# Two of eleven sums in an earlier place, and second readings of a weight in three tiles instead of one

## The chip, the core and the metric

The kernel runs on one core of one Trainium2 chip. The time is the device time of one execution, in microseconds (us). The kernel before took 561.12 us, the median of three runs (560.93 to 561.14). Beside the runs there is one execution recorded by the profiler, with a span of 558.1 us from the first to the last instruction.

The engines are named as in the profile: PE is TensorE (PEld are its weight loads), DVE is VectorE, ACT is ScalarE, POOL is GpSimd, and SP is the queue that issues most transfers. "L685" is line 685 of the kernel.

## What is computed

A gated recurrence over 768 tokens, for 4 batches of 8 heads of 48 values, then two matrix products with a SiLU between them, for 3072 tokens:

```python
for t in range(S):
    state = alpha[:, :, t, :, None] * state + np.einsum('bhd,bhe->bhde', k[:, :, t], v[:, :, t])
    y[:, :, t] = np.einsum('bhd,bhde->bhe', q[:, :, t], state)
...
x = np.ascontiguousarray(attn_out.transpose(0, 2, 1, 3)).reshape(B * S, H * D)   # 3072 x 384
h = x @ w_in                          # 384 x 2048
g = h * (1.0 / (1.0 + np.exp(-h)))
return (g @ w_out).astype(np.float32) # 2048 x 384
```

The weights arrive as 64-bit floats. The kernel reads them as pairs of 32-bit words and makes 32-bit floats of them.

## The kernel before

**Stages.** The tokens are cut into 24 pieces n of 128 (6 chunks of 4 batches), and four pieces form a group: six groups of 512 tokens. A loop of 25 steps, each with four slots, runs the attention of piece n (`scores`, `products`, `quotient`, `values`, `states`, `flip`, `land`). `values` writes the attention's output for two pieces side by side into a tile `xt`, one of the group's two halves. After each slot `fill` issues pieces of the two matrix products, as many as are due by a count of PE's work. A piece in the list `pieces` is a generator, its work, and the number of attention pieces that have to be done (`bridged`) before it may go. In the steps themselves the matmuls keep the order of the text on PE (`keep_in_program_order`); the operations of the other engines are ordered when the program is built, by their dependencies and their place in the text, and only those marked with `keep_in_program_order` stay behind what was written just ahead of them on their engine.

**First product.** `enter_plain` (groups 0 and 1) multiplies as the formula says. `enter` (groups 2 to 5) uses 20 block products in place of more (`PRODUCTS`, pairs of a combination of blocks of w_in and one of x), in seven pieces for each of two pairs of blocks. It needs combinations of blocks of x, which `sums_x` makes with the eleven operations of `SUMS_X` on VectorE; they lie in a tile `xc` of eleven rows, x numbers 6 to 16, of which the first sum writes x 9 and the second x 6. PE's first products of a group read x 9, x 6 and x 6, the fourth x 15, which is the eighth sum. The results are added up in VectorE (L944 and L998) and go through SiLU on ACT (L941).

**Second product.** `leave` takes g of half a group in seven pieces of 16 matmuls. VectorE or ACT add up the blocks and write the result o (L1042, L1040), which a DMA stores. Its two PSUM banks `ps_o` are used in turn.

**Order of pieces.** `both` puts the pieces of `leave` of one group and `enter` of the next in turns. `sums_x` of a group is a piece of no work at the head of its phase. The list `phases` says where a phase ends in `pieces`; `marks` says in which slot.

**Second readings.** `audit` reads alpha, w_in and w_out once more and reduces each piece to its largest (and for the weights smallest) value on VectorE (L685), for a test at the end of whether the fast way was allowed. It has 37 pieces: 9 of alpha (512 KB each), 12 of w_in (512 KB) and 16 of w_out (384 KB). All land in one tile, `bits` of the pool `look`, so that a transfer (L677) waits for the reduction of the one before. A call of the generator reduces one piece and asks for the next; two calls are made in each of the steps 15 to 24, the rest in the loop at L1215, which puts one or two pieces of the matrix products between two calls. Then come the test (`ends`, `good`, `small`, L1225 to L1236), with five pieces of the products in it, four more pieces, the load of the result into a register of each engine (L1239), hints for the branch (L1243), and the rest of the pieces. The slow way (`general`) is not entered.

**Tiles of attention.** `settle` allocates what is used from piece n = 8 on, when the tiles of the start are freed: `look`, `part`, `xc`, `turn`, `wx`, `p`, and the three tiles `at`, `kt` and `qt` (`late["quads"]`, 800 values in each of 128 partitions) into which alpha, k and q of a piece are loaded.

Of the kernel before, what the change touches and what calls it, by code (L numbers as in the profile page):

```python
# [8 lines left out]
F32 = mybir.dt.float32  # L9
I32 = mybir.dt.int32  # L10
# [9 lines left out]
def general(  # L20
# [322 lines left out]
SUMS_X = (  # L343
    (9, 1, 2, 1, 4), (6, 1, 0, 1, 2), (7, 1, 2, 1, 3), (8, 1, 0, 1, 7), (10, -1, 1, -1, 8),
    (11, 1, 5, -1, 10), (12, 1, 4, 1, 11), (15, -1, 0, 1, 12), (16, 1, 1, -1, 15),
    (13, 1, 4, 1, 7), (14, -1, 6, 1, 11),
)
# [8 lines left out]
def quotients(  # L356
# [19 lines left out]
    nc = tc.nc  # L376
    dve, act, gps = nc.vector, nc.scalar, nc.gpsimd

    late = {}
# [14 lines left out]
    B, H, S, D = q.shape  # L394
    C = 128
    NCH = S // C
    NP = H // 2
    HD = H * D
# [6 lines left out]
    GB = 4  # L405
# [3 lines left out]
    TB = GB * C // 2  # L409
    HO = HD // 2  # L410

    def pool(name, bufs=1, space=None):
        kw = {} if space is None else {"space": space}
        return ctx.enter_context(tc.tile_pool(name=name, bufs=bufs, **kw))
# [51 lines left out]
    def load(n, names="akq"):  # L466
        if n == NT:
            return
        c = ctxs.setdefault(n, dict(zip(("ci", "b"), divmod(n, B))))
        b, rows = c["b"], slice(c["ci"] * C, c["ci"] * C + C)  # L470
        for name, src in (("a", alpha), ("k", k), ("q", q)):
            if name not in names:
                continue
            x = src[b, :, rows, :]
            if n < NA:
                c[name] = nat[name][n % NIN]
                nc.sync.dma_start(c[name][:, :, 0:D], x.transpose([1, 0, 2]))
                continue

            c[name] = late["quads"][name]
            for u in range(2):
                for i in range(2):
                    r = 64 * u + 32 * i
                    nc.sync.dma_start(
                        c[name][r : r + 32, 32 * (1 - i) :][:, 0 : 4 * NP * D].rearrange(
                            "p (g c) -> p g c", g=NP),
                        x[u::2].rearrange("h (b j) d -> b h (j d)", j=4))
# [83 lines left out]
    quads = w_in.rearrange("p k (q i c) -> p i k q c", i=4, c=128)  # L573
# [6 lines left out]
    def combine(to, sa, a, sb, b):  # L580
        if sa == sb == 1:
            return dve.tensor_tensor(to, a, b, ALU.add)
        if sa == 1:
            return dve.tensor_tensor(to, a, b, ALU.subtract)
        if sb == 1:
            return dve.tensor_tensor(to, b, a, ALU.subtract)  # L586
        return dve.scalar_tensor_tensor(to, a, -1.0, b, ALU.mult, ALU.subtract)
# [69 lines left out]
    def audit():  # L657


        flat = alpha.rearrange("b h s d -> (b h s d)").rearrange("(p c) -> p c", p=128)  # L660
        todo = [(flat[:, c : c + AW], AW, 0) for c in range(0, flat.shape[1], AW)]
        if wide:
            todo += [(moe_w_in[t * 128 : t * 128 + 128, c : c + 512], 512, 1)
                     for c in range(0, DF, 512) for t in range(NKT)]
            todo += [(moe_w_out[f * 128 : f * 128 + 128, :], HD, 1) for f in range(NFT)]
        for kind in (0, 1):
            n = sum(x[2] == kind for x in todo)
            if n:
                seen.append([fix.tile([128, n], F32, name=f"seen{kind}{i}") for i in range(2)])
        at = [0, 0]  # L670
        for src, n, kind in todo:
            t = late["look"].tile([128, 512, 2], I32, name="bits")
            if kind == 0:
                x = t.rearrange("p n w -> p (n w)")[:, 0:n].bitcast(F32)
                nc.sync.dma_start(x, src)
            else:
                nc.sync.dma_start(t[:, 0:n, :].rearrange("p n w -> p (n w)"), src.bitcast(I32))  # L677
                x = t[:, 0:n, 1]
            yield
            i = at[kind]  # L680
            at[kind] += 1
            for which, op in ((0, ALU.max), (1, ALU.min)):
                if kind == 1 or which == 0:
                    tc.keep_in_program_order(
                        dve.tensor_reduce(seen[kind][which][:, i : i + 1], x, axis=AX, op=op,  # L685
                                          apply_absolute_value=True))

    xts, xcs = {}, {}
# [183 lines left out]
    def block_x(grp, at):  # L872

        if at < 2 * NKT:
            return xts[2 * grp + at % 2][:, at // 2, :]
        return xcs[grp][:, at - 2 * NKT, :]

    def sums_x(grp):
        xcs[grp] = late["xc"].tile([128, len(SUMS_X), TB], F32, name="xc")
        for to, sa, a, sb, b in SUMS_X:  # L880
            tc.keep_in_program_order(
                combine(block_x(grp, to), sa, block_x(grp, a), sb, block_x(grp, b)))
        yield
# [8 lines left out]
    turn = [0, 1, 2]  # L892
# [217 lines left out]
    def group(grp):  # L1110
        return [[(enter(grp, pair), 12, GB * grp + GB)] * 7 for pair in range(2)]

    def output(grp):
        return [[(leave(grp, h), 12, GB * grp + GB)] * 7 for h in range(2)]

    def both(x, y):
        for i in range(max(len(x), len(y))):
            pieces.extend(x[i : i + 1] + y[i : i + 1])

    pieces = []  # L1120
# [4 lines left out]
    phases = [len(pieces)]  # L1125
# [2 lines left out]
    phases.append(len(pieces))  # L1128
    before = output(1)
    for grp in range(2, NG):  # L1130
        pieces.append((sums_x(grp), 0, GB * grp + GB))
        for x, y in zip(before, group(grp)):
            both(x, y)
        phases.append(len(pieces))
        before = output(grp)
# [5 lines left out]
    def go_on():  # L1141

        nonlocal done
        next(pieces[done][0], None)
        done += 1

    audits = audit()
    done, bridged = 0, 0
    STEPS = NT + 1
# [4 lines left out]
    def settle():  # L1154

        first.close()
        late.update(look=pool("look"), part=pool("part"), xc=pool("xc"), turn=pool("turn"),
                    wx=pool("wx").tile([128, 8, NQ, 128], F32, name="wx"))
        quads = pool("quads")
        late["p"] = pool("p").tile([128, NP * W + 1], F32, name="p")  # L1160
        late["quads"] = {name: quads.tile([128, 32 + 4 * NP * D], F32, name=f"{name}t") for name in "akq"}
        for name, t in late["quads"].items():
            gps.memset(t, 1.0 if name == "a" else 0.0)
        load(NA)
# [20 lines left out]
    for step in range(STEPS):  # L1185
        if step == 1:
            load(NIN)
        stages = [[(scores, 1)], [(products, 0)], [(values, 1)], [(states, 1)]]
        if step == 1:

            stages = stages[1::-1] + stages[2:]
        elif step >= NA:
            stages = [[(land, 1), (scores, 1)], [(products, 0)], [(quotient, 0)],
                      [(values, 1), (states, 1), (flip, 0)]]
        for slot, group in enumerate(stages):
            for stage, lag in group:
                n = step - lag
                if not 0 <= n < NT:
                    continue
                stage(n)  # L1200
                if stage is values:
                    bridged = n + 1
                if stage is states and n + 1 + NIN < NA:
                    load(n + 1 + NIN)
                if stage is states and n + NV < NT:
                    load_v(n + NV)
            if step * SLOTS + slot == (NA + 1) * SLOTS - 1:
                x = decayed.rearrange("p (o i c) -> p o i c", o=2, c=C)
                for r, o in later:
                    gps.memset(x[r, o, :, 0:CH], 0.0)  # L1210
            fill(step, slot)
            if step * SLOTS + slot >= NA * SLOTS - 1 and conv_done[1] == NFT and not late:
                settle()
    turns = 0
    while next(audits, 0) is None:  # L1215
        turns += 1
        for _ in range(1 + turns % 2):
            go_on()

    checks = [(least.rearrange("p n j -> p (n j)"), ALU.min, 2.0**-64, ALU.is_gt),  # L1220
              (seen[0][0], ALU.max, 1.0, ALU.is_le)]
# [27 lines left out]
@with_exitstack  # L1249
def kernel(  # L1250
    ctx: ExitStack,
    tc: tile.TileContext,
    q: bass.AP,
    k: bass.AP,
    v: bass.AP,
    alpha: bass.AP,
    moe_w_in: bass.AP,
    moe_w_out: bass.AP,
    out: bass.AP,
):  # L1260


    flag = ctx.enter_context(tc.tile_pool(name="flag", bufs=1))
    small = flag.tile([1, 1], I32, name="small")
    args = (q, k, v, alpha, moe_w_in, moe_w_out, out)
    within = quotients(tc, small, *args)
    with tc.If(within < 1, label="general"):
        general(tc, *args)
# [30 lines left out]
```

## Time and profile before

| what | value |
|---|---|
| time, median of 3 runs | 561.12 us |
| span of the profiled execution | 558.1 us |
| mean clock granted to PE | 0.994 |
| DMA moved in the span | 70.13 MB, 126 GB/s |
| L685, max and min of a piece | 65 operations, 42.5 us busy, 24.0 us idle in front of them |
| L582 to L587 on xc, the sums of x | 44 operations |
| reductions of w_out | 455 to 518 us of the span |
| transfer of a piece of w_out, issue to landing | 3.1 us (median of 32) |
| L1239, load of the register | 479 to 535 ns on each engine |
| last store issued | 554.0 us, waited for until 556.2 us |

The span is that of the recorded execution. The runs contain about 3.0 us more, which lie outside the first and the last instruction. Busy shares are means over the whole span; the stages differ, so idle times are read from the timeline, stage by stage. A line of the timeline gives the start, the duration in us, the engine, the line, the operation, what it writes and reads with shapes, and in brackets the idle time of that engine in front of it with what ended it.

### The profile page before, as it was taken

How to read it: one execution, taken by the hardware profiler on the slowest of the kernel's cores; microseconds unless marked ns; L12 is line 12 of the kernel's file. 1: busy time of each engine (PE TensorE's matmuls, PEld its weight loads, DVE VectorE, ACT ScalarE, POOL GpSimd, SP SyncE). 2: the span in 40 equal slices, each digit the busy share in tenths (PEclk: the TensorE clock that was granted, in tenths of full speed). 3: DMA queues.
4: the chain of work that ended last, by engine and by line, in shares of the span. 5: the costliest groups of instructions: out<-in, count | busy, mean ns of one | idle time of the engine just before them, and what ended most of it. 6: DMA issues, size and time to landing. Idle time of an engine off the chain costs nothing. (4 is left out here: it accounts for less than half of the span.)

```text
span 558.1 us, 12640 instructions
## 1 busy us (share of the span) xinstructions
PE 541.4 (97%) x5026; PEld 488.8 (88%) x5026; DVE 445.1 (80%) x801; ACT 208.4 (37%) x466; POOL 75.9 (14%) x146
## 2 busy tenths in 40 slices
PE   5999999999999999999999999999999999999996
PEld 3788887998899898899999999988998999998996
DVE  5887889974999799997998986998894775857531
ACT  3456643223333243353353353353263341432200
POOL 4100010221211211021021021021121000001000
PEclk9799999999999999999999999999999999999999
DMA  9999861164445525355445654717712122333101
GB/s 218 255 276 177 232 189 40 38 164 108 126 131 136 142 62 134 88 145 157 129 109 142 194 141 115 198 22 179 180 48 84 53 99 95 111 109 106 38 25 32
DMA packets 99220, 70.13 MB, mean 126 GB/s; under 512 B 56272, under 2 KB 88656, under 8 KB 99152
## 3 DMA queue, kind: packets, MB, share of 16 engines
q1 hardware_dynamic: 97232, 65.30, 44.6%
q0 software_dynamic: 1920, 3.93, 2.0%
q8 instruction: 41, 0.67, 0.5%
q14 instruction: 27, 0.22, 0.1%
HBM read 61.34 MB, written 7.86 MB: 124 GB/s over the span
## 5 line engine op out<-in xcount | busy, mean ns | idle before, releaser
L388 PE MATMUL ps_o<-w_out,g 128*128 128x192 f32 x768 | 134.7, 329 | 1.1 <-DVE o L1042 0.9
L388 PEld LDWEIGHTS ps_o<-w_out,g 128*128 128x128 f32 x768 | 125.4, 190 | 5.1 <-DVE o L1042 2.3
L388 PE MATMUL ps_m<-xt,w_in 128*128 128x256 f32 x480 | 113.6, 383 | 1.5 <-ACT xt L851 1.1
L388 PEld LDWEIGHTS ps_m<-xt,w_in 128*128 128x128 f32 x480 | 89.1, 190 | 14.4 <-ACT xt L851 1.6
L388 PE MATMUL ps_o<-wt,g 128*128 128x192 f32 x576 | 99.7, 326 | 0.0
L388 PEld LDWEIGHTS ps_o<-wt,g 128*128 128x128 f32 x576 | 95.1, 190 | 1.6 <-issue 0.2
L388 PE MATMUL ps_m<-xc,w_in 128*128 128x256 f32 x288 | 70.7, 382 | 0.0
L685 DVE TENSOR_REDUCE seen<-bits 128x1 f32<-128x384 int32 (+2 forms) x65 | 42.5, 689 | 24.0 <-DMA bits<-in_moe_w_out_dram 19.6
L388 PEld LDWEIGHTS ps_m<-xc,w_in 128*128 128x128 f32 x288 | 53.6, 190 | 7.0 <-DVE g L944 0.3
L941 ACT ACTIVATE g<-g 128x1024 f32<-128x1024 f32 x32 | 33.0, 1056 | 59.0 <-DVE g L944 59.0
L1033 DVE TENSOR_TENSOR g<-g 128x512 f32<-128x512 f32 x72 | 49.8, 708 | 6.1 <-PE ps_o L388 6.1
L1045 POOL DMA_DIRECT2D out_dram<-o x40 | 22.0, 550 | 223.2 <-DVE o L1042 127.6
L813 POOL TENSOR_SCALAR_AFFINE_SELECT g<-g 64x256 f32<-64x256 f32 x64 | 34.2, 534 | 124.8 <-ACT g L806 105.8
L388 PE MATMUL ps_m<-xc,wx 128*128 128x256 f32 x192 | 50.0, 383 | 1.0 <-DVE xc L586 1.0
L936 ACT COPY g<-ps_m 128x512 f32<-128x512 f32 x64 | 36.5, 588 | 36.5 <-PE ps_m L388 36.4
L388 PEld LDWEIGHTS ps_m<-xc,wx 128*128 128x128 f32 x192 | 35.2, 190 | 5.3 <-ACT u L1064 1.3
L944 DVE TENSOR_TENSOR g<-ps_m,g 128x512 f32<-128x512 f32 x56 | 37.0, 684 | 2.9 <-PE ps_m L388 2.7
L722 DVE TENSOR_TENSOR_SCAN u<-al,one 128x516 f32<-128x516 f32 x24 | 30.0, 1249 | 10.6 <-ACT al L719 10.3
L909 ACT ACTIVATE g<-ps_m 128x512 f32<-128x512 f32 x32 | 19.1, 596 | 42.8 <-PE ps_m L388 42.3
L936 ACT COPY part<-ps_m 128x512 f32<-128x512 f32 x32 | 18.9, 589 | 43.0 <-DVE g L944 21.3
L752 DVE TENSOR_TENSOR_SCAN p<-al,inv 128x516 f32<-128x516 f32 x24 | 29.9, 1246 | 1.0 <-PE ps_a L388 0.4
L388 PE MATMUL ps_a<-g,vn 128*32 128x128 f32 x768 | 27.5, 278 | 1.8 <-POOL g L801 1.7
(126 smaller groups left out, 611.4 us busy)
## 6 DMA issues: line engine op xcount, KB each, us to landing
bits<-in_moe_w_in_dram SPq DMA_DIRECT2D x24, 512.0 KB, 4.8
bits<-in_moe_w_out_dram SPq DMA_DIRECT2D x32, 384.0 KB, 3.1
at<-in_alpha_dram SPq DMA_DIRECT2D x64, 96.0 KB, 2.5
kt<-in_k_dram SPq DMA_DIRECT2D x64, 96.0 KB, 2.5
qt<-in_q_dram SPq DMA_DIRECT2D x64, 96.0 KB, 2.6
bits<-in_alpha_dram SPq DMA_DIRECT2D x9, 512.0 KB, 3.8
out_dram<-o POOLq DMA_DIRECT2D x40, 96.0 KB, 2.4
flips<-turn SPq DMA_DIRECT2D x12, 256.0 KB, 2.4
```

Source lines behind the costliest of these rows:

```text
L388: in_order(nc.tensor.matmul(*args, **kw))
L685: dve.tensor_reduce(seen[kind][which][:, i : i + 1], x, axis=AX, op=op, apply_absolute_value=True))
L722: dve.tensor_tensor_scan(u[:, end - 1 :: -1], sg[:, end:0:-1], one[:, end:0:-1], 0.0, ALU.mult, ALU.add)
L752: dve.tensor_tensor_scan(p[:, 0:end], sg[:, 0:end], iv[:, 0:end], 0.0, ALU.mult, ALU.add)
L813: gps.affine_select(x, x, pattern=[[0, NP], [1, CH]], compare_op=ALU.is_ge, fill=0.0, base=0, channel_multiplier=-1)
L909: act.activation(gts[grp, h, pair][:, i : i + 2, q % 2, :], ps, AF.Silu)
L936: act.copy(to, ps)
L941: act.activation(x, x, AF.Silu)
L944: dve.tensor_tensor(to, a, b, op)
L1033: dve.tensor_tensor(cells(grp, h, pair, *to), cells(grp, h, pair, *x), cells(grp, h, pair, *y), ALU.subtract)
L1045: (gps if grp < NG - 1 else nc.sync).dma_start(out[r : r + C, c * HO : (c + 1) * HO], o)
```

## The change

`sums_x` is a generator with two parts now: it yields ahead of its third sum. The first part is a piece of its own, two places ahead of the end of the phase before, and may go when two of the group's four attention pieces are done; the rest stands where all the sums stood. `xc` is one tile for all groups, allocated in `settle`, where each group had a new one of the same pool.

In `audit`, a piece whose data fit into a tile of 800 values (only those of w_out do, with 768) lands in `at`, `kt` or `qt` in turn, and up to two further pieces are asked for ahead of the reduction of one. The pieces of alpha and w_in land in `look` as before, one at a time. The last loop puts one piece of the products between two calls, where it put two and one in turn.

```diff
@@ audit
+        assert 2 * HD <= 32 + 4 * NP * D
         todo = [(flat[:, c : c + AW], AW, 0) for c in range(0, flat.shape[1], AW)]
...
+        alone = sum(2 * x[1] > 32 + 4 * NP * D or x[2] == 0 for x in todo)
...
         at = [0, 0]
-        for src, n, kind in todo:
-            t = late["look"].tile([128, 512, 2], I32, name="bits")
+        landed = []
+
+        def begin(src, n, kind):
+            at = len(landed)
+            t = late["look"].tile([128, 512, 2], I32, name="bits").rearrange("p n w -> p (n w)") if (
+                at < alone) else late["quads"]["akq"[at % 3]].bitcast(I32)
             if kind == 0:
-                x = t.rearrange("p n w -> p (n w)")[:, 0:n].bitcast(F32)
-                nc.sync.dma_start(x, src)
+                landed.append(t[:, 0:n].bitcast(F32))
+                nc.sync.dma_start(landed[-1], src)
             else:
-                nc.sync.dma_start(t[:, 0:n, :].rearrange("p n w -> p (n w)"), src.bitcast(I32))
-                x = t[:, 0:n, 1]
+                nc.sync.dma_start(t[:, 0 : 2 * n], src.bitcast(I32))
+                landed.append(t[:, 0 : 2 * n].rearrange("p (n w) -> p n w", w=2)[:, :, 1])
+
+        for i, (src, n, kind) in enumerate(todo):
+
+            while len(landed) < min(i + (1 if i + 1 < alone else 3), len(todo)):
+                begin(*todo[len(landed)])
+            x = landed[i]
             yield
@@ sums_x
-        xcs[grp] = late["xc"].tile([128, len(SUMS_X), TB], F32, name="xc")
-        for to, sa, a, sb, b in SUMS_X:
+        xcs[grp] = late["xc"]
+        for i, (to, sa, a, sb, b) in enumerate(SUMS_X):
+            if i == 2:
+                yield
@@ the list of pieces
     for grp in range(2, NG):
-        pieces.append((sums_x(grp), 0, GB * grp + GB))
+        sums = sums_x(grp)
+        pieces.insert(len(pieces) - 2, (sums, 0, GB * grp + 2))
+        phases[-1] += 1
+        pieces.append((sums, 0, GB * grp + GB))
@@ settle
-        late.update(look=pool("look"), part=pool("part"), xc=pool("xc"), turn=pool("turn"),
+        late.update(look=pool("look"), part=pool("part"), turn=pool("turn"),
+                    xc=pool("xc").tile([128, len(SUMS_X), TB], F32, name="xc"),
@@ the last loop
-    turns = 0
     while next(audits, 0) is None:
-        turns += 1
-        for _ in range(1 + turns % 2):
-            go_on()
+        go_on()
```

## The prediction

> **What bounds the kernel now.** I read the page first, for the busy shares: TensorE decides.
>
> ```profile
> span 558.1 us, 12640 instructions
> PE 541.4 (97%) x5026; PEld 488.8 (88%) x5026; DVE 445.1 (80%) x801; ACT 208.4 (37%) x466; POOL 75.9 (14%) x146
> ```
>
> The reader is to see that whatever is to be won has to come out of idle time of PE: VectorE at 80% has slack on average, but not in every stage. The second view is the timeline of the weight loads (PEld), because each matmul here needs its own load of about 190 ns, and a gap in front of a load is a gap in the whole stream. After 144 us, leaving out gaps of at most 0.33 us (most of them the sequencer's own), these are the gaps that stand in the groups and the final loop:
>
> ```profile
> 219.37 0.73 PEld L388 LDWEIGHTS ps_m<-xt,wx 128*128 128x128 f32 x4 [1.32 <-DVE g L944]
> 230.72 0.73 PEld L388 LDWEIGHTS ps_m<-xt,w_in 128*128 128x128 f32 x4 [0.81 <-DVE g L944]
> 369.73 0.73 PEld L388 LDWEIGHTS ps_m<-xc,wx 128*128 128x128 f32 x4 [1.29 <-ACT u L1064]
> 479.23 2.57 PEld L388 LDWEIGHTS ps_o<-w_out,g 128*128 128x128 f32 x16 [0.47 <-DVE o L1042]
> 515.67 1.27 PEld L388 LDWEIGHTS ps_o<-w_out,g 128*128 128x128 f32 x8 [1.11 <-DVE o L1042]
> 517.36 1.27 PEld L388 LDWEIGHTS ps_o<-w_out,g 128*128 128x128 f32 x8 [0.41 <-ACT g L941]
> 535.35 2.57 PEld L388 LDWEIGHTS ps_o<-w_out,g 128*128 128x128 f32 x16 [0.48 <-DVE o L1042]
> ```
>
> With one of 0.32 at 229.18 (also on L944) they come to 6.2 us: 2.45 in group 2 (219 to 231), 1.29 at the start of group 4, 0.47 + 1.11 + 0.41 around the final loop, 0.48 after it. That is the most that this change can win. The gap at 369.73 is named after ACT, but the timeline of PE puts the same gap (1.02) on the sum of L586, and that sum runs 369.22 to 369.62 on VectorE: the sum is what ended last.
>
> Third view, VectorE's share in the stages that hold these gaps (columns: PE, PEld, DVE, ACT, POOL busy, clock, DMA share, GB/s):
>
> ```profile
> 188.40:231.00 42.60, 41.25 (x413) 37.26 (x402) 41.84 (x83) 14.59 (x38) 5.68 (x11) 1.00 0.39 103
> 349.50:369.70 20.20, 19.24 (x209) 17.47 (x207) 20.17 (x39) 8.47 (x20) 4.00 (x6) 1.00 0.57 149
> 447.70:494.30 46.60, 46.53 (x252) 43.44 (x251) 32.49 (x63) 16.34 (x29) 2.69 (x5) 1.00 0.32 105
> ```
>
> VectorE is full in groups 2 (98%) and at the start of group 4 (99.9%), and free in the final loop (70%). Last, VectorE's own timeline: an idle place ahead of group 2's sums, and the end of group 5's first half:
>
> ```profile
> 188.43 0.69 DVE L1019 TENSOR_TENSOR g<-g 128x512 f32<-128x512 f32 x1 [2.49 <-ACT g L909]
> ...
> 505.72 1.01 DVE L685 TENSOR_REDUCE seen<-bits 128x1 f32<-128x384 int32 x2 [2.46 <-DMA bits<-in_moe_w_out_dram]
> ...
> 509.64 1.01 DVE L685 TENSOR_REDUCE seen<-bits 128x1 f32<-128x384 int32 x2 [0.91 <-DMA bits<-in_moe_w_out_dram]
> ...
> 513.75 1.00 DVE L685 TENSOR_REDUCE seen<-bits 128x1 f32<-128x384 int32 x2
> 514.67 0.68 DVE L587 SCALAR_TENSOR_TENSOR g<-g 128x512 f32<-128x512 f32 x1
> 515.27 0.35 DVE L1042 TENSOR_TENSOR o<-ps_o,u 128x192 f32<-128x192 f32 x1
> ```
>
> The reductions of the second reading (L685) stand in front of L1042, which frees the bank that PE waits for at 515.67.
>
> **What the Trainium skill says.** "Perfetto Trace Analysis", Identifying the Most-Contended Engine: matmul busy is a poor measure, the share of LDWEIGHTS a good one. The trace agrees: PE reads 97% where PEld, whose gaps I use, reads 88%. "DVE: scalar operands, raw-bit mode, write accounting and state across instructions", Flops that outlive an instruction: VectorE has one in-order queue. The trace agrees: at 505.72 it sat 2.46 us for a transfer and then ran the L944 behind it. [...]for the 384 KB of a piece of w_out; the trace has a median of 3.1 from issue to landing, and that is what I use. "Runtime: NRT & Kernel Launch", Instruction fetch mechanics: a taken branch to a page that isn't held stalls for its fetch; in the trace before the closing branches took 64 to 397 ns, so no such stall shows.
>
> **Part 1, sums.** Per group 2 to 5, the first two of the eleven sums (rows for x 9 and 6, 1.05 to 1.10 us for three in a row, so about 0.75 for two) move ahead of the last pieces of the group or phase before. Nothing is added: the same instructions, no DMA. They need only the first half of the group's tokens, which the condition GB * grp + 2 says. They overwrite rows that the group before reads last in its products 12 and 14 of 20, two pieces earlier on PE, so the new place should wait for nothing. The third sum writes x 7, still read by product 18, and stays where it was.
>
> Group 2: VectorE runs without a gap from 188.43 on and PE waits for it three times, 2.45 us in all. The two sums now fit in the 2.49 us of idle time before 188.43. Everything behind them comes 0.75 earlier, until PE's own pace is what counts: gain 0.75 if the gaps shrink one for one. I take 0.7; bounds 0 and 1.0.
> Groups 3 and 5: no gap of PE at their starts; 0. The moved sums delay the L1042 and L944 at the end of the group before by 0.75. At group 4's start, the nearest case I can measure, L1042 ends at 358.39 and its bank is wanted at 359.66, and the L944 at 358.30 (two, 1.29) free banks wanted at 363.29: covers of 1.3 and 3.7 us, both above 0.75. Cost 0; 0.4 per group if that cover is smaller elsewhere.
> Group 4: here VectorE has no idle time between 349.5 and 369.7 in which to hide the two sums, so what is done earlier pushes the rest back by the same 0.75, and the eighth sum, for which PE waits, ends when it did. I take 0. Bounds: the whole 1.29 gained, if the build's order (which puts a scan of 1.43 us and a transpose of 1.10 between these sums) turns out kinder; 0.5 lost, if worse.
> xc being one tile and not a new one per group takes no time of its own.
>
> **Part 2, second readings.** 37 pieces (9 of alpha, 12 of w_in, 16 of w_out), 20 of them asked for in steps 15 to 24 (two a step). The final loop thus has 17 turns. Before, a turn alternates two pieces and one: 9 x 2 + 8 = 26 pieces of PE's work. After, 17. A piece is 2.6 us of PE (16 matmuls of leave from 510.48 to 513.08, 12 of enter from 507.89 to 510.48), so the last reduction moves 9 x 2.6 = 23.4 us up, from 518 to about 494.5, in front of the critical end of group 5. SP's issues: still 16 transfers, 0.33 us each on a queue that holds nothing else until the stores at 524.5; each now waits for the reduction of three pieces before.
> The wait for landing: issue two pieces ahead is 5.2 us against 3.1, so the 19.6 us of VectorE's waits on w_out go. They are off PE's path except at the end.
> Load between 447.7 and 494.3: 32.49 busy before, with 10 of the 16 w_out pairs in it; six more at 1.01 make 38.6 of 46.6, 83%. Before, busy plus blocked on landings was 32.5 + 11.9 = 44.4, 95%, and PE lost only 0.47 there. So the denser reductions should cost PE nothing; if the cover is gone, see the rival below.
> End of group 5's first half: without the reduction of 1.00 at 513.75, and with VectorE free at 508.7 and 512, L587, L1042 and the two L944 all come about 1.0 earlier. The bank of L1042 is then late by no more than the 0.48 which stands at 535.35 and the 0.47 at 479.23, where the same change of output comes with no reduction in front: 1.11 - 0.48 = 0.63. SiLU (L941) comes 1.0 earlier too, so the 0.41 at 517.36 goes. Gain 1.04; bounds 0.4 and 1.2. Next late is that same 0.48.
> The gap at 479.23 stays. The closing test moves 9 pieces up: eight small operations (about 1 us of VectorE in all) and the load of the register (479 to 535 ns on each engine) fall at about 495 to 503, among pieces that use VectorE and ACT. Cost 0.1; bounds 0 and 0.6, cover being the pace of PE. The hint for the branch comes 9 pieces sooner; if it were lost, the fetch lies beside the last store, for which SP waits from 554.4 to 556.2. I take 0, bounds 0 and 1.5.
>
> **Sum.** -0.7 - 1.04 + 0.1 = -1.65 us. On the span of 558.1, 556.45; around it lie 561.12 - 558.1 = 3.0 us that stay. Against the median of the runs: 559.5.
>
> **Rivals.**
> Only half of it shows (0.25): moved sums help nothing, because group 2's order is built anew and PE's gaps move to other instructions, while the end wins 0.6. For it: PE's gaps in group 2 are on L944, not on a sum. Against: VectorE is saturated there, and it is its total that counts. 560.5, within 560.0 to 561.5.
> More (0.10): group 4's 1.29 goes too. For it: PE waits there for a sum by name. Against: no idle time to move into. 559.5 - 1.3 = 558.2.
> Slower (0.17): reductions no longer wait for a transfer and crowd the final loop, standing in front of the L944 that free PE's banks. Group 2 shows the price of that with VectorE at 98%: 2.45 us in 42.6. Over the loop's 46.6 us it is +2.7; the end still wins 1.0, the sums nothing: 562.8. It decides from +2.8 us of new gaps in the loop on, against forecast gains of 1.7 and the 1.1 that is told from no change. For it: 1.01 us blocks in an in-order queue, one per 2.6 us. Against: 83%, less than the 95% before.
>
> **How the numbers follow.** About 0.2% (1.1 us) can be told from no change. Forecast, 558.9 to 560.3: 0.48, of which 0.43 is faster by that. With the larger gain 0.10 and 0.03 of the half case, faster is 0.56; same is 0.05 + 0.22 + 0.01 = 0.28; slower 0.16. The range 557.9 to 561.9 leaves out most of the slower case and the end of the larger gain, some 0.18.
>
> **What would show it.** Part 1: the gaps at 219 to 231 shrink to about 1.7 in all; two sums of xc stand in VectorE's timeline before 188; the gap at group 4's start is about 1.3. Part 2: no wait of L685 on w_out; last L685 near 495; the gap of 1.11 is near 0.5, that of 0.41 is gone. Wrong: new gaps of PE on L944 or L1042 between 447 and 495, a wait of a first sum on PE, or a gap at the registers' load near 503.

## The result and the profile after

The changed kernel took 557.18 us, median of six runs (556.59 to 558.02); the kernel before 560.73, median of six, of which three are the runs named at the top and three were run beside it. The ratio is 0.9943, with an interval of 0.9926 to 0.9959, so the gain is 3.2 us (2.3 to 4.1) by the ratio. Forecast was a gain of 1.62 and a time of 559.5, not below 557.9: the direction was right, the gain twice the forecast.

The page of the kernel after, its span and busy shares:

```profile
span 555.5 us, 12640 instructions
PE 541.4 (97%) x5026; PEld 489.7 (88%) x5026; DVE 445.4 (80%) x801; ACT 208.5 (38%) x466; POOL 76.1 (14%) x146
```

PE's and VectorE's busy times are what they were: the work is the same, and the 2.6 us between the two spans are idle time of PE. Line numbers have moved: L685 is L697 now, L944 is L958, L1042 is L1056, L941 is L955, L1033 is L1047, L696 is L708. The timeline of the weight loads after, with the gaps of groups 2 to 5 and the final loop:

```profile
227.92 0.73 PEld L388 LDWEIGHTS ps_m<-xc,w_in 128*128 128x128 f32 x4 [0.30 <-DVE g L958]
229.45 0.73 PEld L388 LDWEIGHTS ps_m<-xt,w_in 128*128 128x128 f32 x4 [0.79 <-DVE g L958]
368.35 0.73 PEld L388 LDWEIGHTS ps_m<-xc,wx 128*128 128x128 f32 x4 [1.23 <-ACT u L1078]
501.11 0.09 PEld L388 LDWEIGHTS ps_a<-ones,good 128*1 128x1 f32 x2 [0.23 <-issue]
532.31 2.57 PEld L388 LDWEIGHTS ps_o<-w_out,g 128*128 128x128 f32 x16 [0.80 <-DVE o L1056]
```

Of the seven gaps shown of before, four are gone: 1.32 at 219, 0.47 at 479, 1.11 and 0.41 at 516 and 517. The 0.81 at 230 and the 1.29 at 369 are still there (0.79 and 1.23). The one after the loop grew from 0.48 to 0.80: before, 18 matmuls on `wt` run ahead of that gap and 14 behind it, after it is 16 and 16, so two matmuls that covered some 0.3 of it now come later. The closing test's matmul at 501.11 has 0.23 on PE's sequencer in front of it and no wait; before, at 526.66, it had the same 0.23.

VectorE's timeline after, at the places that the prediction named:

```profile
182.84 0.96 DVE L582 TENSOR_TENSOR xc<-xt 128x256 f32<-128x256 f32 x2
...
188.38 0.69 DVE L1033 TENSOR_TENSOR g<-g 128x512 f32<-128x512 f32 x1 [1.63 <-ACT g L923]
...
476.44 0.35 DVE L1056 TENSOR_TENSOR o<-ps_o,u 128x192 f32<-128x192 f32 x1
476.71 1.01 DVE L697 TENSOR_REDUCE seen<-kt 128x1 f32<-128x384 int32 x2
...
489.47 1.00 DVE L697 TENSOR_REDUCE seen<-at 128x1 f32<-128x384 int32 x2
```

The two sums stand at 182.84, and the idle time ahead of 188.4 has shrunk from 2.49 to 1.63: they were paid for out of it. At 476 a reduction stands directly behind the L1056 that frees PE's bank. The last reduction is at 489.47. The load of the loop, by windows (columns as in the prediction):

```profile
447.70:494.30 46.60, 46.60 (x255) 43.91 (x254) 38.07 (x78) 16.69 (x28) 2.70 (x5) 1.00 0.44 132
```

VectorE is busy 38.07 of 46.60 us, and PE lost nothing there.

### The profile page after: what moved, and what is told of

Its sections match the earlier page's. It is cut to its first block, busy times and chain, and to the rows that moved or that the text cites. A ratio compares the mean times of both kernels' runs of the same rounds, so it can differ in the third digit from the quotient of the medians.

```text
span 555.5 us, 12640 instructions
## 1 busy us (share of the span) xinstructions
PE 541.4 (97%) x5026; PEld 489.7 (88%) x5026; DVE 445.4 (80%) x801; ACT 208.5 (38%) x466; POOL 76.1 (14%) x146
## 5 line engine op out<-in xcount | busy, mean ns | idle before, releaser
L1047 DVE TENSOR_TENSOR g<-g 128x512 f32<-128x512 f32 x72 | 50.1, 709 | 8.3 <-PE ps_o L388 8.3
L955 ACT ACTIVATE g<-g 128x1024 f32<-128x1024 f32 x32 | 33.1, 1056 | 61.2 <-DVE g L958 61.1
L958 DVE TENSOR_TENSOR g<-ps_m,g 128x512 f32<-128x512 f32 x56 | 37.1, 683 | 3.2 <-PE ps_m L388 2.7
L697 DVE TENSOR_REDUCE seen<-bits 128x1 f32<-128x512 int32 (+1 forms) x33 | 26.3, 823 | 5.7 <-DMA bits<-in_moe_w_in_dram 5.7
L1056 DVE TENSOR_TENSOR o<-ps_o,u 128x192 f32<-128x192 f32 x24 | 8.5, 355 | 25.7 <-PE ps_o L388 22.8
```

The source lines that it names most:

```text
L955: act.activation(x, x, AF.Silu)
L958: dve.tensor_tensor(to, a, b, op)
L1047: dve.tensor_tensor(cells(grp, h, pair, *to), cells(grp, h, pair, *x), cells(grp, h, pair, *y), ALU.subtract)
L1056: dve.tensor_tensor(o, x, y, ALU.add)
```

## The experiments

The prediction's theory of the end was that a reduction of 1.00 us stands in front of L1042, and that the new pace moves it away. The rival was that the transfer is what counts: one tile makes a closed chain (reduce, ask, land, reduce) with a period of its own, on which VectorE's in-order queue sits. Then the groups' sums, the second readings as a load, and the two gaps that stayed were taken one at a time. Ratios are against the kernel before, run beside each of them on the same chip. Its median was 560.57 us beside the runs of the first two parts, 560.39 beside `before_again`, `no_second_w_out`, `other_bank` and `sums_first_g4`, and 559.16 on the chip of the other three; so times are compared only beside the same median, and ratios elsewhere.

### Each part alone

`sums_only` is the kernel before with part 1 (`sums_x` in two pieces, one tile `xc`); `audit` and its loop are those of before:

```diff
...
-        pieces.append((sums_x(grp), 0, GB * grp + GB))
+        sums = sums_x(grp)
+        pieces.insert(len(pieces) - 2, (sums, 0, GB * grp + 2))
+        phases[-1] += 1
+        pieces.append((sums, 0, GB * grp + GB))
...
```

> Leaves the second readings as before (one tile, two and one piece in turn), keeps the moved sums. If the moved sums are worth what the trace shows in group 2 (gaps of PE from 2.45 to 1.09 us) and nothing else: 1.3 to 1.4 us faster than before, span near 556.7, the gaps of 0.47, 1.11 and 0.41 at the end of groups 4 and 5 still there. Rival, that the sums win nothing by themselves and the order of the whole program was only shaken up: within 0.4 us of before.

`readings_only` has the rest of the diff (`begin`, the three tiles, one piece a turn) and the sums of before:

```diff
...
+            while len(landed) < min(i + (1 if i + 1 < alone else 3), len(todo)):
+                begin(*todo[len(landed)])
...
     while next(audits, 0) is None:
-        turns += 1
-        for _ in range(1 + turns % 2):
-            go_on()
+        go_on()
```

> Leaves the sums as before, keeps the second readings ahead in three tiles and one piece a turn. If the two parts add up: 1.5 to 1.7 us faster than before (0.47, 1.11 and 0.41 of gaps gone, 0.3 given back at 535), the gaps of 1.32 at 219 and 1.29 at 369 as before. Rival, that they do not add up (the sums' gain came with the new order of the readings): 2.5 us or more faster, or less than 0.8.

Measured: 559.27 us for the sums, ratio 0.9976 (0.9966 to 0.9986), a gain of 1.3; 558.15 for the readings, 0.9950 (0.9933 to 0.9967), a gain of 2.8. The loads of the sums alone:

```profile
217.00 0.73 PEld L388 LDWEIGHTS ps_m<-xt,wx 128*128 128x128 f32 x4 [0.37 <-DVE g L946]
...
477.35 2.57 PEld L388 LDWEIGHTS ps_o<-w_out,g 128*128 128x128 f32 x16 [1.01 <-DVE o L1044]
...
514.61 1.27 PEld L388 LDWEIGHTS ps_o<-w_out,g 128*128 128x128 f32 x8 [1.66 <-DVE o L1044]
```

The gap of group 2 is down to 0.37, but those of the second readings read 1.01 and 1.66, where before they were 0.47 and 1.11. What the sums win at 217 could seem lost again at the end. Whether it was the sums that did this is what `before_again` settles below. With the readings alone, PE has no gap from 477 to 517 but the 0.23 at the closing test's matmul. The two gains add up to 4.1, where both together won 3.2, and 2.8 lies in the range that was put down for parts that do not add up. The intervals (0.8 to 1.9, and 1.8 to 3.8) leave room for either; the table after `g2_sums_late` settles it by stretches.

### Pace, or tiles

`ahead_old_pace` is the kernel after with two pieces and one in turn again, so that the reductions stand where they stood; `new_pace_one_tile` is the kernel after with the `audit` of before, so one piece a turn and one tile:

```diff
@@ ahead_old_pace, against after
+    turns = 0
     while next(audits, 0) is None:
-        go_on()
+        turns += 1
+        for _ in range(1 + turns % 2):
+            go_on()
@@ new_pace_one_tile, against after
-            while len(landed) < min(i + (1 if i + 1 < alone else 3), len(todo)):
-                begin(*todo[len(landed)])
-            x = landed[i]
+            t = late["look"].tile([128, 512, 2], I32, name="bits")
...
+                nc.sync.dma_start(t[:, 0:n, :].rearrange("p n w -> p (n w)"), src.bitcast(I32))
+                x = t[:, 0:n, 1]
```

> As the changed kernel, but with two pieces and one in turn again in the last loop, so the reductions still reach to the end of group 5, with no wait for landings. If it is the wait for a transfer in front of L1056 that held PE: as fast as the changed kernel within 0.3 us. If it is the reduction itself standing in front of L1056 at the end of group 5: 0.8 to 1.4 us slower than the changed kernel, with a gap near 1 us at 513.

> As the changed kernel, but the second readings land in one tile again, with one piece a turn. A turn then takes some 4.0 us (3.1 of transfer and 1.0 of reductions) against 2.6 us of PE's work. If the prefetch is what makes the new pace possible: VectorE is held up by (4.0 - 2.6) x 16, some 22 us in all, PE shows new gaps, 5 to 20 us slower than the changed kernel. Rival, that VectorE's work can wait that long since PE has slack: within 1 us of the changed kernel.

Measured: 556.80 us for the first, ratio 0.9929 (0.9913 to 0.9945), as good as the change itself; 577.77 for the second, 1.0306 (1.0287 to 1.0325), 17 us slower than before and some 20 slower than the change by the ratios, just above the 5 to 20 that were expected. VectorE with the tiles ahead and the old pace, at the end of group 5's first half:

```profile
510.35 0.68 DVE L587 SCALAR_TENSOR_TENSOR g<-g 128x512 f32<-128x512 f32 x1
511.56 0.36 DVE L1056 TENSOR_TENSOR o<-ps_o,u 128x192 f32<-128x192 f32 x1 [0.52 <-PE ps_o L388]
511.83 1.00 DVE L697 TENSOR_REDUCE seen<-at 128x1 f32<-128x384 int32 x2
```

Reductions run in this stretch as they did before, and VectorE still has 0.52 us to wait for PE ahead of L1056: no gap is left at 479 or 513. (0.41 remains at 514.66, on SiLU, and the gap after the loop is 0.48, as before, where the new pace has 0.80; so the two paces come out level.)

With the data ahead the build also puts a reduction behind this L1056, so the order could be the cause and not the wait. The lines just ahead of these answer that. VectorE with the tiles ahead:

```profile
505.00 1.00 DVE L697 TENSOR_REDUCE seen<-kt 128x1 f32<-128x384 int32 x2
506.37 0.36 DVE L1099 TENSOR_TENSOR u<-ps_o,u 128x192 f32<-128x192 f32 x1 [0.37 <-PE ps_o L388]
...
507.04 1.00 DVE L697 TENSOR_REDUCE seen<-qt 128x1 f32<-128x384 int32 x2
```

and in the kernel before, where this line comes right behind the reduction at 509.64, for whose data VectorE had waited 0.91:

```profile
510.57 0.35 DVE L1085 TENSOR_TENSOR u<-ps_o,u 128x192 f32<-128x192 f32 x1
```

Both have one reduction ahead of L1085 (L1099) and one more between it and the L1042 (L1056) that frees the bank. From start to start that stretch takes 4.70 us before, and 5.19 less 0.52 of waiting, 4.67, with the tiles ahead: the work is the same. What is gone is the wait for the landing, and L1099 now waits for PE. At 479 the last reduction even stands in the same place, in front of L587 and L1056 (474.30 with the tiles ahead, 477.31 before), and no gap is left there either; before, VectorE had waited 1.01 us for the data of the reduction at 473.33. So neither moving the reductions up nor taking one away from in front of L1056 was needed; having their data there was.

The one tile at the new pace, loads and VectorE:

```profile
519.44 0.09 PEld L388 LDWEIGHTS ps_a<-ones,good 128*1 128x1 f32 x2 [17.67 <-DVE good L1234]
```

```profile
509.48 1.01 DVE L685 TENSOR_REDUCE seen<-bits 128x1 f32<-128x384 int32 x2 [2.88 <-DMA bits<-in_moe_w_out_dram]
513.59 1.01 DVE L685 TENSOR_REDUCE seen<-bits 128x1 f32<-128x384 int32 x2 [3.09 <-DMA bits<-in_moe_w_out_dram]
517.78 1.01 DVE L685 TENSOR_REDUCE seen<-bits 128x1 f32<-128x384 int32 x2 [3.18 <-DMA bits<-in_moe_w_out_dram]
```

Here the chain shows its period: 4.1 to 4.2 us from reduction to reduction, 1.0 of work and some 3.1 of transfer. PE's pieces in a turn are 2.6 us, so the chain falls back by 1.5 us a turn, and nearly the whole debt comes due at one place (a gap of 0.92 stands at 478.44): the closing test's matmul, for which PE's queue waits 17.67 us in order. In the kernel before, 26 pieces in 17 turns are 26 x 2.6 / 17 = 4.0 us a turn. The old pace was thus almost exactly the chain's period: two clocks, PE and the chain, side by side, neither with slack on the other.

### Before once more

`before_again` is the kernel before, unchanged, for a second profile of it.

> The kernel before once more, unchanged, so its ratio to the kernel before shows what the comparison resolves. If runs differ mainly at the start (loads of the first 50 us): ratio 1.000 within 0.002, gaps of PE after 130 us as in the first profile to within 0.1 us. If the first profile of before was not typical of its later stages: other gaps, and about 1 us more of them.

Measured: 560.06 us, ratio 0.9995 (0.9983 to 1.0007); its profile has a span of 559.0 where the first had 558.1. Its loads:

```profile
479.36 2.57 PEld L388 LDWEIGHTS ps_o<-w_out,g 128*128 128x128 f32 x16 [0.95 <-DVE o L1042]
...
516.44 1.27 PEld L388 LDWEIGHTS ps_o<-w_out,g 128*128 128x128 f32 x8 [1.65 <-DVE o L1042]
```

The same program, and the two gaps of the readings read 0.95 and 1.65 in place of 0.47 and 1.11: one microsecond more, about the 0.9 between the spans. The waits of VectorE for w_out come to 22.1 us (longest 3.0) where the first profile had 19.6 (2.5). The longest wait for a landing is half a microsecond longer, in a chain without slack, and PE pays. So the larger gaps of `sums_only` are not the sums' doing: they stand in before as well, in another execution.

### The readings as a load, and group 2's sums

`no_second_w_out` is the kernel after without the 16 second readings of w_out (the test then says nothing of w_out); `g2_sums_late` puts only group 2's early sums back:

```diff
@@ no_second_w_out
-            todo += [(moe_w_out[f * 128 : f * 128 + 128, :], HD, 1) for f in range(NFT)]
@@ g2_sums_late
-        pieces.insert(len(pieces) - 2, (sums, 0, GB * grp + 2))
-        phases[-1] += 1
+        if grp > 2:
+            pieces.insert(len(pieces) - 2, (sums, 0, GB * grp + 2))
+            phases[-1] += 1
+        else:
+            pieces.append((sums, 0, GB * grp + GB))
```

> As the changed kernel, with the 16 second readings of w_out left out altogether (so the closing test covers alpha and w_in only). If the three tiles have taken these readings off PE's path entirely: as fast as the changed kernel within 0.4 us. If they still cost something (VectorE's 16 us of reductions among the additions of group 5, transfers): 0.8 us or more faster.

> As the changed kernel, but group 2's two sums stand where they stood before; those of groups 3 to 5 are moved. If all of the sums' gain comes from group 2: a gap of 1.0 to 1.3 us is back near 219, and it is 1.0 to 1.4 us slower than the changed kernel. If the order of the rest matters as much: within 0.5 us of it.

Measured: 557.21 us without the readings, ratio 0.9945 (0.9929 to 0.9962): the same as with them. With group 2's sums late, 557.79 us, 0.9971 (0.9959 to 0.9983), and the gap is back:

```profile
219.12 0.73 PEld L388 LDWEIGHTS ps_m<-xt,wx 128*128 128x128 f32 x4 [1.32 <-DVE g L958]
```

The ratio is 0.0028 above that of the change, 1.6 us, though the two intervals reach 0.0012 and 0.0017 to either side. The profiles tell the stretches apart. In the table the marks are starts of the same three blocks of loads of the attention (`ps_a<-g,vn`; in before at 187.69, 231.78 and 441.76), and the end is that of VectorE's last addition:

| kernel | first mark at | group 2, to the second mark | to the third | to the end |
|---|---|---|---|---|
| `before` | 187.69 | 44.09 | 209.98 | 112.19 |
| `before_again` | 187.21 | 43.82 | 210.37 | 113.31 |
| `sums_only` | 186.27 | 43.14 | 209.93 | 113.54 |
| `readings_only` | 188.03 | 44.09 | 210.16 | 110.81 |
| `ahead_old_pace` | 187.07 | 43.14 | 210.16 | 110.88 |
| `after` | 187.64 | 42.87 | 209.91 | 110.81 |
| `no_second_w_out` | 185.83 | 42.86 | 210.00 | 110.81 |
| `g2_sums_late` | 187.44 | 44.08 | 209.94 | 110.81 |

The sums shorten group 2 and nothing else that stands out of the spread; the tiles ahead shorten the last stretch, at either pace, to what it takes without any second readings of w_out. Read ahead, 16 reductions of 1.0 us and 16 transfers cost PE nothing. So the parts do add up, each in its own stretch. And the first mark, ahead of which no part does anything but the first two sums, moves by 2.2 us between profiles.

### The gap after the loop

`other_bank` is the kernel after with the outputs of the last half group begun on the other PSUM bank, so that an output no longer follows on the bank that VectorE is still reading:

```diff
...
     def out_bank(i, n):
-        return outs[i].tile([128, 512], F32, name="ps_o")[:, 0:n]
+        return outs[(i + swap[0]) % 2].tile([128, 512], F32, name="ps_o")[:, 0:n]
@@ leave
+        swap[0] = int(grp == NG - 1 and h == 1)
```

> As the changed kernel, but the last half group's output starts on the other PSUM bank, so that its first piece does not follow the seventh of the one before on the same bank. If the gap of 0.80 at 532 is the wait for that bank alone: the gap gone, 0.5 to 0.8 us faster than the changed kernel. If something else is late next there (the SiLU or the additions in front of the first product): no more than 0.2 us.

Measured: 556.22 us, ratio 0.9931 (0.9913 to 0.9950), span 554.4; the loads at that place:

```profile
528.87 2.30 PEld L388 LDWEIGHTS ps_o<-wt,g 128*128 128x128 f32 x14
531.15 1.98 PEld L388 LDWEIGHTS ps_o<-w_out,g 128*128 128x128 f32 x12
```

Nothing in brackets ahead of 531.15: the gap of 0.80 is gone. The median is 1.0 us below that of `no_second_w_out`, which ran beside it, though the intervals of the two overlap; the last stretch of the table takes 110.04 here, 0.77 less than in the change. At 479 and 515 an `enter` piece of eight matmuls (1.73 us) lies between the two outputs; at 532 nothing does. That is why this gap stayed and those could go.

### The gap of group 4

Three tries on the 1.23 at 368. `sums_first_g4` holds the attention's operations of step 21 (the scan and the transposes) behind the group's last sum; `bank_and_skip` is `other_bank` with the four second readings of steps 20 and 21 moved into the last loop; `bank_and_pool` is `other_bank` with the two early sums on GpSimd:

```diff
@@ sums_first_g4
...
+                if stage is products and step == 5 * GB + 1:
+                    with tc.issue_after(late["sum"]):
+                        stage(n)
...
@@ bank_and_skip
-        if at % 2 == 0 and step > 3 * GB + 2:
+        if at % 2 == 0 and step > 3 * GB + 2 and step // 2 != 5 * GB // 2:
@@ bank_and_pool
+            if i < 2:
+                gps.tensor_tensor(block_x(grp, to), block_x(grp, a), block_x(grp, b), ALU.add)
...
```

> As the changed kernel, but in the step at group 4's start the attention's scan and transposes stay behind the eleven sums on VectorE. If the gap of 1.23 at 368 is the eighth sum kept back by that scan (1.43) and the transposes and products among the sums: the gap gone, 0.9 to 1.2 us faster than the changed kernel. If VectorE is simply full there, as the prediction held: the gap stays or another takes its place within 10 us, no gain.

> As other_bank, and the four second readings asked for in steps 20 and 21, around group 4's start, go to the last loop instead (same readings, later). If VectorE is simply full at group 4's start: taking 2.6 us of reductions out ahead of it and among it lets the eighth sum come in time, the gap of 1.24 at 368 goes and does not come back at 392 to 402, 1.0 to 1.3 us faster than other_bank. If the order of the sums among the attention's operations alone decides: the gap stays.

> As other_bank, with the two early sums of each group on GpSimd. If VectorE's total is the limit at group 4's start: 0.75 us less there, gap of 1.24 down to about 0.5, 0.5 to 0.9 us faster than other_bank. Rival, that GpSimd at work stretches VectorE's operations (as 0.42 to 0.62 us beside the selections): no gain, or slower.

Measured: 557.37 us, ratio 0.9943 (0.9923 to 0.9963), for the first, no better than the change. Its loads:

```profile
392.54 0.73 PEld L388 LDWEIGHTS ps_m<-xt,wx 128*128 128x128 f32 x4 [1.02 <-DVE g L958]
...
398.57 0.73 PEld L388 LDWEIGHTS ps_m<-xt,w_in 128*128 128x128 f32 x4 [0.98 <-DVE g L958]
```

The 1.23 at 368 is gone, and 1.02 and 0.98 have come 24 to 30 us later: on this full engine another order only chose where PE waits. On GpSimd the two sums brought nothing either: 556.47 us, 0.9948 (0.9935 to 0.9961), where `other_bank` has 0.9931; the gap at 367 is 1.32, and gaps of 0.56 and 0.33 stand at 392 and 398 that `other_bank` does not have.

With the four readings moved, the gap at 368 went and did not come back at 392 to 402, so it is a matter of load. But the time was 559.15 us, 0.9991 (0.9977 to 1.0005), the gain of the change gone, where 1.0 to 1.3 us less than `other_bank` had been expected. The loads in its last loop:

```profile
477.08 0.73 PEld L388 LDWEIGHTS ps_m<-xt,w_in 128*128 128x128 f32 x4 [1.48 <-DVE g L960]
478.87 4.25 PEld L388 LDWEIGHTS ps_o<-w_out,g 128*128 128x128 f32 x16 [1.05 <-DVE o L1058]
```

The pieces moved are of w_in, which land in the one tile and hold up those behind them; VectorE was busy without a break from 474 to 481, with a reduction at 477.55 right in front of the L1058 that frees PE's bank. And the 16 loads at 478.87 took 4.25 us where after has 2.68. The runs of this kernel spread widely, from 555.61 to 560.76 (before beside it: 557.37 to 560.40), as if the chain and PE were level again; no run takes that apart.

## Why the prediction was wrong, point by point

**The step that failed.** It is the last stretch. The prediction put the waits for landings off PE's path, left the gap at 479 standing and took 0.48 of the 1.11 at 515 for a floor; it expected 1.04 to be won, less 0.1 for the closing test. By the table that stretch won 1.4 us against the first profile and 2.5 against `before_again`. The term of group 2 was too small beside it, by about 0.5. (The stated terms add up to 1.64, not 1.65, which changes nothing.)

**Group 2: right mechanism, term too small.** The sums fit into VectorE's idle time as said, and the gap at 219 went. Forecast 0.7, bounds 0 and 1.0; by the runs it is 1.3 (`sums_only`) to 1.6 (`g2_sums_late`), by the table 0.7 to 1.2, and 1.2 between the first profile and the change. The term missing: besides two sums fewer (0.7 from start to start), sums behind them ran faster. Three of the group's sums took 0.62 us before (at 194.89 to 195.99) beside GpSimd's selections at 194.31; in the change two of these three take 0.42. Every profile without the early sums has these three at 0.62, and every one with them has one of the three. That is 0.4. The scan u took 1.49 before (at 217.11) and 1.23 after, but 1.23 in `before_again` and 1.48 in `sums_only` too: these 0.26 go with the execution and not with the change, and they are the difference between 1.32 and 1.06 of gap at 219. GpSimd's four selections beside the scan took 1.84 in the first profile, and 2.85 and 2.87 in the two with the short scan. "SBUF — State Buffer", Who interferes with whom, says that a VectorE instruction with two inputs in SBUF contends with a GpSimd instruction that reads SBUF. The trace agrees in the main, 0.42 against 0.62 for the same operation, though of the two moved sums, both beside selections that began at 180.62, one takes 0.42 and one 0.63; no run here took GpSimd's work away, so this share of the gain is argued, not shown.

**"The gap at 479.23 stays": wrong.** The floor of 0.48, taken from 535.35, was carried to 479 and 515, where other neighbours stand. There an `enter` piece lies between the outputs, and the floor is 0; both gaps went entirely. `other_bank` shows that 535's has a cause of its own. The step "1.11 - 0.48 = 0.63" should have been 1.11, and 0.47 at 479 was to be won too; against that, 0.3 was lost at 532.

**The cause of the end's gain: the wrong step.** The prediction put it on the reductions being moved 23.4 us up. They were, and further (last one 489.47, forecast 494.5), but `ahead_old_pace` wins as much without it, and with a reduction still between L1099 and L1056. It said of the waits for landing that they are "off PE's path except at the end"; in truth the chain of one tile, 4.1 us a turn, ran beside PE's 4.0, and the last of its waits, 1.01 us at 473.33 and 0.91 at 509.64, are what made VectorE late for both places, 479 and 515. `new_pace_one_tile` shows the same chain where it decides alone.

**The base, and what one profile can say.** The sum carried 3.0 us around the span, the median of three runs less the span of a fourth; and not all of that lies outside the first and the last instruction, though the text on the profile before says so. Where one execution has both numbers, 1.7 to 1.9 us lie around the span (557.26 and 555.5 for after, 560.75 and 559.0 for `before_again`). So some 1.2 of the 3.0 were the spread between executions, which for the kernel before reaches from 558.8 to 562.9 us on one chip. The forecast gain doesn't rest on it, but the gaps that it adds up carry the same spread: from the first mark of the table to the end, after is 2.7 us shorter than the first profile and 3.9 shorter than `before_again`, and 3.2 (2.3 to 4.1) was measured. `sums_only`, whose readings are those of before, is near `before_again` in the last stretch; which of the two is nearer to the typical run stays open.

**What was right.** Groups 3 and 5 win nothing that can be told from the spread. Group 4 wins nothing: VectorE is full there, and an order changed by hand moved the gap and did not remove it. 83% of load in the loop makes no gap: 38.07 us measured, 38.6 forecast. No reduction waits for w_out any more. The closing test shows no cost: 0.23 in front of its matmul before and after. The slower rival (crowding in front of L944) didn't happen with w_out's pieces read ahead; `bank_and_skip`, with more of w_in's in one tile, comes near to it: there the gaps are on L960 (L944 before) and L1058.

## What to carry to other kernels

A transfer into one tile and the work that frees it form a chain with a period; compare that period (here 4.1 us) with the pace of the bound engine (4.0) before calling its waits hidden, and when they are equal, take two profiles, because here half a microsecond of landing time showed at PE. A gap measured at one place is the floor only of places with the same neighbours. And on the engine that was full for a stage, reordering moved a gap; less work in the stage, or idle time ahead of it, removed one. And when executions differ by as much as the change is worth, compare profiles by stretches between marks that every kernel has, not by their spans.

## What was not expected of the hardware

Here PE's clock fell after idle time, and the price came behind the gap. The windows of `new_pace_one_tile` (the column behind POOL is the granted clock):

```profile
502.00:506.00 4.00, 0.07 (x1) 0.00 (x0) 1.03 (x3) 0.00 (x0) 0.54 (x1) 1.00 0.38 123
508.00:519.00 11.00, 0.00 (x0) 0.00 (x0) 3.24 (x9) 0.00 (x0) 0.00 (x0) 0.50 0.31 99
519.44:523.00 3.56, 3.56 (x10) 2.90 (x11) 0.84 (x2) 0.58 (x1) 0.00 (x0) 0.50 0.01 2
524.00:530.00 6.00, 6.00 (x34) 5.64 (x33) 3.44 (x8) 1.53 (x2) 0.54 (x1) 1.00 0.06 19
```

Full clock for the first 4 us of idleness, half clock later, and half clock for some 4 us of work after PE has resumed: by an estimate from these, about 2 us on top of the 17.67. "TensorE: Matmul & The Clock Gate", What's actually happening, tells of half the rate after an idle window of about 3.4 us and of full rate after a busy one; this run agrees. `bank_and_skip` lost half its clock without such a window of idleness. Its windows:

```profile
476.00:479.40 3.40, 1.67 (x8) 1.21 (x8) 3.40 (x8) 1.06 (x1) 0.29 (x1) 0.97 0.47 147
479.40:482.60 3.20, 3.20 (x12) 3.20 (x12) 3.18 (x6) 1.64 (x2) 0.25 (x1) 0.50 0.84 244
```

PE was never idle for 3.4 us, only half busy (1.67 of 3.40) through two gaps close together, and lost half its clock for the next 3.2 us all the same. In `before_again` the gaps of 1.65 and 0.41 at 516 left the clock at 1.00.
